# Late score step: sixteen pooled products of 32 columns first, the local products behind them

## The chip, the cores and the metric

The kernel runs on one core of one Trainium2 chip. The metric is device time in microseconds of one execution; the median of three runs is compared. Five engines matter: TensorE (PE, with its weight loads shown apart as PEld), VectorE (DVE), ScalarE (ACT), GpSimd (POOL), and SyncE (SP), which here only starts DMAs.

## The reference

Inputs q, k and v are 8 batches x 8 heads x 576 positions x 64. For each head there are two attentions that are added, and a feed-forward layer follows:

```
q_d, k_d, v_d = means over groups of 4 positions        # 144 pooled positions
out_d     = softmax(q_d k_d^T / 8) v_d                  # 144 x 144 scores, repeated 4 times
out_local = softmax(q k^T / 8 where |i - j| < 4) v      # a band of 7 positions
x = out_up + out_local                                  # 4608 tokens x 512
out = (h * cos(h)) @ w_out,  h = x @ w_in               # 512 -> 2048 -> 512
```

## The kernel before, in words

Most of the time goes to the feed-forward layer. It works on 12 tiles of 384 tokens and 16 blocks of 128 hidden units, with every float32 operand split into two float16 parts; line 1574 (and line 1499 later in the program) is its first product, line 1594 its second. Between those products stand the attention steps, one unit for each of 8 batches and 4 pairs of heads. Units of the first two batches are handled by other functions. The 24 units of batches 2 to 7 are "late" and have three steps each: scores (`late_s`), transposes (`late_t`) and the product with v (lines 1378 and 1385).

A late score step gets q and k of two heads (64 partitions each, so one head per half of the array's rows), and `qkd`, the sums of q and of k over groups of four positions, 144 of each. It computes into two PSUM banks, one per head:

- 48 local products at line 1071: 24 segments of 24 queries, each 32 query columns (stationary) by 32 key columns (moving), for two heads. Each falls on a piece of the array of 64 rows x 32 columns.
- 4 pooled products at line 1078: for each head all 144 pooled queries against 144 keys. The stationary operand has at most 128 columns, so the 144 queries are covered by two products, `i = 0` and `i = 1`, of 128 columns each. They overlap: of the second only the last 32 queries of a head are used, and the column offset is shifted by 32 for the second head so that these land on other partitions (`P - 32..P` for head 0, `64..96` for head 1).

All operands are float32. A float32 product is shown in the trace as two LDWEIGHTS and two MATMUL records, so 48 products are 96 records and 4 are 8.

The readers of the two banks stand on VectorE: line 1087 adds the band mask to the local scores, line 1101 takes the maxima of the pooled scores, line 1097 subtracts them. `late_t` then transposes the pooled weights (line 1130) and sends them through DRAM with small DMAs of SyncE (line 1135 and the line behind it). The next q and k are loaded by line 814 on SyncE's queue into the buffers that a score step has read; there are two of each.

The order on every engine is written out ahead of time by a planner (class `Plan`). It gives each operation a cost in us, simulates the engines, and disturbs the order by a table of seeds (`PICKS`). The score step is one operation for it, of cost 1.55 and with `num=209` instructions; neither number changes here. What a function like `mm` issues inside one operation is not the planner's matter.

Of the kernel before, what the change touches and what calls it, by code (L numbers as in the profile page):

```python
# [28 lines left out]
P = 128  # L29
# [11 lines left out]
SD = S // 4  # L41
# [3 lines left out]
BQ, BS = 24, 32  # L45
# [12 lines left out]
REM = SD - P  # L58
# [460 lines left out]
def _dve(n):  # L519
    return n * 0.001042 + 0.065  # L520
# [7 lines left out]
def attn_ffn_kernel(ctx: ExitStack, tc: tile.TileContext, qT, kT, vdn, vl, w_in, w_out, out, small):  # L528
# [4 lines left out]
    pe, act, dve, pool, sp = nc.tensor, nc.scalar, nc.vector, nc.gpsimd, nc.sync  # L533
# [9 lines left out]
    def sb(tag, n, shape, dtype=F32, name=None, pool=None):  # L543
        t = pl.turn(tag, n)
        if small and t in GUEST:
            k, c, off = GUEST[t]
            host, size = words[(k, c)], math.prod(shape[1:])
            pl.rings.setdefault(t, host)

            def make():  # L550
                half = host.get().rearrange("p f t -> p (f t)")[:, DM:].bitcast(dtype)
                return half[:shape[0], off:off + size]
            return pl.buf(make, t)
        return pl.buf(lambda: (pool or ap).tile(shape, dtype, name=name or tag, tag=t, bufs=1), t)
# [227 lines left out]
    def ub(b, pr, name):  # L782
        shape, n, chunk, off = UNIT[name]
        if b >= NEARLY and name in ("ptd", "vd4", "vd"):
            shape = [KH[0]] + shape[1:]
        if b == 1 and pr and name in "qk":

            own = cut(xx[1], 584 * (name == "k"), shape) if pr == 1 else \
                cut(wx[{(2, "q"): ("o", 8), (2, "k"): ("i", 7), (3, "q"): ("o", 7), (3, "k"): ("o", 6)}[(pr, name)]], 0, shape)
            return own  # L790
        if b < NEARLY and pr:
            return cut(wx[OWN[5 * (NPAIR - 1 - pr) + chunk]], off, shape)
        return sb({"ptl": "sml", "xs": "vd4"}.get(name, name), 2 if name == "ptl" else n, shape)

    def bank(b, kind):

        if b == 0:
            tags = ("pa.0", "po.0", "pa.1", "po.1") if kind == "s" else ("ph.0", "ph.1", "pa.2")
            return psum(tags[int(pl.turn("early" + str(kind == "s"), len(tags))[-1])])
        return psum(pl.turn("pa", 3) if b < NEARLY else pl.turn("pa", 2))  # L800
# [246 lines left out]
    def late_s(b, pr, u, q, k, qkd):  # L1047


        banks = [bank(b, "s") for _ in range(2)]  # L1050
# [7 lines left out]
        sml, smd = ub(b, pr, "sml"), pl.buf(lambda: prob, "prob")  # L1058
        loc, poo = [pl.buf(None) for _ in banks], [pl.buf(None) for _ in banks]

        def using(bk, o):
            bk.r.append(o)
            bk.acc.append(o)

        def mm():
            for f in range(2):
                for n in range(NSEG):
                    for g in range(4):
                        h = (g // 2 + f) % 2
                        hs, o, c = slice(64 * h, 64 * h + 64), (4 * n + g) * BQ, LQ + BS * n  # L1070
                        pe.matmul(banks[h].get()[BS * g:BS * (g + 1), c:c + BS],  # L1071
                                  q.get()[hs, o:o + BS], k.get()[hs, o:o + BS], start=True, stop=True)
            for i in range(2):
                for h in range(2):
                    hs = slice(64 * h, 64 * h + 64)
                    at = (SD - P + BS * h) * i
                    few = qkd.get()[hs].rearrange("p a n -> p (a n)")[:, at:at + P]
                    pe.matmul(banks[h].get()[:, i * SD:(i + 1) * SD], few, qkd.get()[hs, 1, :], start=True, stop=True)  # L1078
        pl.op("PE", 1.55, mm, r=[q, k, qkd], pw=banks, w=loc + poo, slack=SLACK, num=209)

        mxl, su, nl = sb("mxl", 2, [P, 2 * NSEG]), sb("su", 2, [P, 2 * NSEG + 3]), 2 * NSEG
        n = 2 * NSEG * BS
# [12 lines left out]
        def less(h, out, cols, r, lo, hi, **kw):  # L1095
            n = (cols.stop - cols.start) * SD
            using(banks[h], pl.op("DVE", _dve(n), lambda: dve.tensor_tensor(
                out=out(), in0=dq(h)[lo:hi, cols], in1=mxd.get()[lo:hi, h, cols].unsqueeze(2).broadcast_to([hi - lo, n // SD, SD]),
                op=ALU.subtract), r=[poo[h], mx[h]] + r, pw=[smd], **kw))
# [3 lines left out]
        wide0 = pl.buf(None)  # L1103
        less(0, lambda: smd.get()[:, 0::2, :SD], slice(0, 2), [], 0, P, w=[wide0])
        less(1, lambda: smd.get()[:, 1:2, :SD], slice(0, 1), [], 0, P)
        less(1, lambda: smd.get()[2 * BS:3 * BS, 2:3, :SD], slice(1, 2), [wide0], 2 * BS, 3 * BS)
        m = 3 * SD
        ds = lambda: smd.get()[:, :, :SD]

# [15 lines left out]
    def late_t(b, pr, u):  # L1125

        sml, smd = u["sml"], u["smd"]
        ptl, ptd, trn = ub(b, pr, "ptl"), ub(b, pr, "ptd"), sb("smd", 1, [P, 3, SD + REM], name="trn")
        scr = sb("scr", 2, [2, SD + REM, SD], pool=dr)
        pl.op("DVE", _dve(3 * (SD + REM)), lambda: dve.transpose(trn.get().rearrange("p s q -> p (s q)"),  # L1130
                                                                smd.get().rearrange("p s n -> p (s n)")), r=[smd], w=[trn])

        def out_():
            for g in range(4):
                sp.dma_start(scr.get().rearrange("h (j k) q -> k (h j) q", k=BS)[:, :, BS * g:BS * (g + 1)],
                             trn.get()[BS * g:BS * (g + 1), :2].rearrange("p h (j q) -> p (h j) q", q=BS))
            for h in range(2):
                sp.dma_start(scr.get()[h, :, P:].rearrange("(j k) q -> k j q", k=BS),
                             trn.get()[BS * (3 - h):BS * (4 - h), 2].rearrange("p (j q) -> p j q", q=BS)[:, :, BS - REM:])

        def in_():
            for i, lo in enumerate((0, KH[0])):
                sp.dma_start(ptd.get()[:KH[i], i], scr.get()[:, lo:lo + KH[i]].rearrange("h k q -> k h q"))
        pl.op("SP", 6 * 0.55, out_, r=[trn], w=[scr], lat=2.2)
        pl.op("SP", 2 * 0.55, in_, r=[scr], w=[ptd], lat=3.8)
        pl.op("DVE", _dve(2 * NSEG * BS), lambda: dve.transpose(ptl.get().rearrange("p s q -> p (s q)"),
                                                                sml.get().rearrange("p s n -> p (s n)")), r=[sml], w=[ptl])
        u["ptb"] = pl.buf(lambda: ptb, "ptb")

        def move():  # L1150
            for g in range(4):
                sp.dma_start(ptb[BS * g:BS * (g + 1), g % 2], ptl.get()[BS * g:BS * (g + 1)])
        dma(8 * P * NSEG * BS, move, r=[ptl], w=[u["ptb"]])
        u["ptl"], u["ptd"] = ptl, ptd

    def u_s(b, pr, part=None):
# [5 lines left out]
        if b >= NEARLY:  # L1162
            return late_s(b, pr, u, q, k, qkd)
# [632 lines left out]
```

## Time and profile before

| what | before |
|---|---|
| three runs, us | 905.36, 907.74, 912.56; median 907.74 |
| the profiled execution, its own time | 906.36 us |
| its span, first to last instruction | 904.4 us |
| granted TensorE clock, mean | 0.998 |
| PE busy | 876.5 us, 97% |
| DVE, ACT, POOL busy | 724.8, 625.5, 451.9 us |
| chain that ended last | PE 58%, DVE 14%, ACT 11%, POOL 4% |
| code fetched for PE | 84 packets, 1.38 MB |

The busy time of an engine is a union of its records, so it does not tell how well a busy PE is used. The chain that ended last is followed back from the last instruction: what stands on it sets the end, as far as the profile's semaphores tell. Records of one line that overlap are merged into one row in the timeline, with the time from the first start to the last end; the start of the row behind it tells when the engine went on.

### The profile page before, as it was taken

The numbers are of one execution on the slowest core, as the hardware profiler recorded it, in microseconds if no ns is written. First come the engines' busy times: TensorE is split into PE (matmuls) and PEld (weight loads), VectorE is DVE, ScalarE is ACT, GpSimd is POOL, SyncE is SP. The second block draws the span as 40 slices with busy tenths as digits, with TensorE's granted clock in tenths as the row PEclk, the third lists the DMA queues.
The fourth block names the chain that finished last, engine by engine and source line by source line (L and its number), as shares of the span: only waits on it lengthen the run. The fifth ranks groups of instructions, "written<-read, shape, count | busy, mean of one in ns | idle before, by whom it ended". The sixth has DMA issues, their size and how long they took to land.

```text
span 904.4 us, 26251 instructions
## 1 busy us (share of the span) xinstructions
PE 876.5 (97%) x10488; PEld 575.2 (64%) x10488; DVE 724.8 (80%) x1596; ACT 625.5 (69%) x1370; POOL 451.9 (50%) x563
## 2 busy tenths in 40 slices
PE   8989899999999999999999999999999999999996
PEld 4745555455555555777776667677776677777773
DVE  6889887999886959877789889977789878857662
ACT  3889999956666566566676766676686776655653
POOL 4694754557664636544367626533347534522221
PEclk9999999999999999999999999999999999999999
DMA  7893285115364731322424532334454421224501
GB/s 231 257 294 88 92 283 202 42 40 96 86 142 118 151 99 63 96 52 74 130 70 118 145 105 87 89 93 121 134 129 119 116 62 55 79 75 141 175 1 40
DMA packets 100853, 103.80 MB, mean 115 GB/s; under 512 B 47280, under 2 KB 73648, under 8 KB 100720
## 3 DMA queue, kind: packets, MB, share of 16 engines
q1 hardware_dynamic: 99280, 99.40, 37.5%
q0 software_dynamic: 1296, 2.36, 1.9%
q8 instruction: 84, 1.38, 0.6%
q14 instruction: 49, 0.40, 0.2%
q10 hardware_dynamic: 144, 0.26, 0.1%
HBM read 81.05 MB, written 16.22 MB: 108 GB/s over the span
## 4 chain that ended last, share of the span: by engine, by line
PE 58%; DVE 14%; ACT 11%; POOL 4%; issue 3%; DMA 1%; DVEq 0%; SPq 0%; ACTq 0%; POOLq 0%
PE bank L1594 27%; PE bank L1499 17%; PE bank L1574 8%; DVE rec L1415 3%; PE bank L1071 2%; PE bank L1385 2%; PE bank L1378 1%; ACT xxh L730 1%; PE bank L1078 1%; ACT tr L1554 1%; DVE tr L1555 1%; POOL wdo L678 1%; ACT L1554 1%; DVE tr L1552 1%; ACT xxh L726 1%
## 5 line engine op out<-in xcount | busy, mean ns | idle before, releaser
L1499 PEld LDWEIGHTS <-wdi 128*128 128x128 f16 x2400 | 204.3, 98 | 58.1 <-issue 4.1
L1594 PE MATMUL bank<-wdo,gh 128*128 128x512 f16 x696 | 207.1, 379 | 0.0
L1499 PE MATMUL bank<-wdo,wdi 128*128 128x192 f16 x1344 | 141.0, 246 | 2.1 <-DVE wdo L1520 1.4
L1594 PE MATMUL bank<-wdo,gl 128*128 128x512 f16 x348 | 131.7, 379 | 0.1
L1574 PEld LDWEIGHTS <-wdi 128*128 128x128 f16 x768 | 73.9, 98 | 58.8 <-issue 2.4
L1594 PEld LDWEIGHTS <-gh 128*128 128x128 f16 x696 | 64.0, 98 | 41.3 <-issue 0.2
L1594 PE MATMUL bank<-wdo,wdi 128*128 128x512 f16 x342 | 86.6, 379 | 0.7 <-ACT wdi L1612 0.7
L1554 ACT ACTIVATE tr<-tr,quarter 128x384 f32<-128x384 f32 x98 | 59.8, 613 | 39.3 <-DVE tr L1552 38.9
L678 POOL TENSOR_TENSOR gl<-tr,gh 128x384 f16<-128x384 f32 x51 | 49.9, 978 | 73.6 <-ACT gh L1557 39.4
L1594 PE MATMUL bank<-wdo,wdo 128*128 128x512 f16 x315 | 79.8, 379 | 1.5 <-ACT ob L1612 1.5
L1594 PEld LDWEIGHTS <-gl 128*128 128x128 f16 x348 | 34.1, 98 | 41.5 <-POOL gl L678 0.6
L1594 PEld LDWEIGHTS <-wdo 128*128 128x128 f16 x342 | 32.2, 98 | 29.0 <-issue 2.0
L1594 PEld LDWEIGHTS <-wdi 128*128 128x128 f16 x342 | 32.3, 98 | 28.4 <-issue 2.1
L1551 ACT ACTIVATE tr<-bank 128x384 int32<-128x384 f32 x66 | 31.6, 479 | 21.9 <-DVE bank L1515 16.9
L1555 DVE SCALAR_TENSOR_TENSOR tr<-tr,bank 128x384 f32<-128x384 f32 x66 | 35.9, 544 | 13.2 <-ACT tr L1554 13.1
L1415 DVE TENSOR_TENSOR rec<-rec 128x128 f32<-128x128 f32 (+1 forms) x98 | 44.3, 456 | 1.9 <-POOL rec L1415 0.7
L1515 DVE TENSOR_TENSOR bank<-bank,wdo 128x384 f32<-128x384 f32 x64 | 35.7, 558 | 12.0 <-PE bank L1499 11.7
L1554 ACT ACTIVATE wdo<-wdo,quarter 128x384 f32<-128x384 f32 x47 | 28.8, 613 | 20.8 <-DVE wdo L1552 20.6
L1121 POOL TENSOR_TENSOR blocks<-blocks,su 128x432 f32<-128x432 f32 x22 | 21.1, 959 | 43.8 <-DVE su L1118 37.6
L678 POOL TENSOR_TENSOR wdo<-rec,wdo 128x384 f16<-128x384 f32 (+1 forms) x34 | 34.1, 1010 | 17.5 <-ACT wdo L1460 16.4
L678 POOL TENSOR_TENSOR gl<-wdi,gh 128x384 f16<-128x384 f32 x26 | 25.2, 969 | 32.4 <-ACT gh L1557 22.7
L1554 ACT ACTIVATE wdi<-wdi,quarter 128x384 f32<-128x384 f32 x47 | 28.8, 613 | 17.4 <-DVE wdi L1552 17.2
(421 smaller groups left out, 2349.9 us busy)
## 6 DMA issues: line engine op xcount, KB each, us to landing
vl<-vl SPq DMA_DIRECT2D x26, 384.0 KB, 3.4
vd<-vdn SPq DMA_DIRECT2D x24, 384.0 KB, 4.7
wdi<-w_in SPq DMA_DIRECT2D x16, 512.0 KB, 5.6
wdo<-w_out SPq DMA_DIRECT2D x16, 512.0 KB, 7.1
again<-w_in SPq DMA_DIRECT2D x32, 256.0 KB, 4.8
again<-w_out SPq DMA_DIRECT2D x32, 256.0 KB, 3.6
q<-qT SPq DMA_DIRECT2D x26, 292.0 KB, 3.6
k<-kT SPq DMA_DIRECT2D x26, 292.0 KB, 4.2
```

The source lines that it names most:

```text
L678: f = lambda e: lambda: e.tensor_tensor(out=out(), in0=in0(), in1=in1(), op=ALU.subtract)
L1071: pe.matmul(banks[h].get()[BS * g:BS * (g + 1), c:c + BS], q.get()[hs, o:o + BS], k.get()[hs, o:o + BS], start=True, stop=True)
L1121: f = lambda e, get=get, by=by: lambda: e.tensor_tensor(out=get(), in0=get(), in1=by(), op=ALU.mult)
L1385: pe.matmul(banks[e].get()[64 * h:64 * h + 64, o:o + 2 * BQ], v4[r, NSEG * h + n, :], pt[r, :, NSEG * h + n, :BQ], start=True, stop=True)
L1415: f = lambda e: lambda: e.tensor_tensor(out=out(), in0=in0(), in1=in1(), op=op)
L1499: pe.matmul(bank.get()[:, half * HT:(half + 1) * HT], w(i, a), x(l, a), start=start and k == 0, stop=k == 5, skip_group_check=not start)
L1515: pl.op("DVE", _dve(TT), lambda: dve.tensor_tensor(out=by.get()[:, :TT], in0=by.get()[:, :TT], in1=s.get(), op=ALU.add), r=[mid, s], w=[by])
L1551: pl.op("ACT", _act(m, banked), lambda: act.activation(turns(), h(), AF.Copy, scale=1.0 / fm.h, bias=0.25), r=r, w=[tr])
L1554: pl.op("ACT", _act(m, False, 1), lambda: act.activation(tr.get(), tr.get(), AF.Sin, scale=-2.0 * PI / fm.h, bias=quarter), w=[tr], tab="sin")
L1555: pl.op("DVE", _dve(m), lambda: dve.scalar_tensor_tensor(out=tr.get(), in0=tr.get(), scalar=-0.5 * fm.ratio, in1=h(), op0=ALU.mult, op1=AL ...
L1574: pe.matmul(ph.get()[:, :m], w[:, i, kc, :], x[:, kc, :], start=(n == 0), stop=(n == 3 * KC - 1))
L1594: pe.matmul(o, (gh, gh, gl)[k].get()[:, sl], wo.get()[:, (0, 1, 0)[k]], start=(c == c0 and k == 0), stop=(c == c1 - 1 and k == 2))
```

## The change

In `late_s` the pooled products come first and are cut differently: for each head, four of 32 stationary columns cover the first 128 queries, and four more, all with the same last 32 queries, stand for the second range. That makes 16 products, each on a piece of the array of 64 rows x 32 columns, the same pieces that the local products use. The 48 local products follow, unchanged. Since the last 32 queries now lie on all four groups of partitions, head 1's are taken from partitions 32 to 63 and head 0's from 0 to 31, and `late_t` sends them from there.

```diff
         def mm():
+            for i in range(2):
+                for g in range(4):
+                    for h in range(2):
+                        hs, at = slice(64 * h, 64 * h + 64), SD - BS if i else BS * g
+                        pe.matmul(banks[h].get()[BS * g:BS * (g + 1), i * SD:(i + 1) * SD], qkd.get()[hs, 0, at:at + BS], qkd.get()[hs, 1, :],
+                                  start=True, stop=True)
             for f in range(2):
                 for n in range(NSEG):
                     for g in range(4):
...
-            for i in range(2):
-                for h in range(2):
-                    hs = slice(64 * h, 64 * h + 64)
-                    at = (SD - P + BS * h) * i
-                    few = qkd.get()[hs].rearrange("p a n -> p (a n)")[:, at:at + P]
-                    pe.matmul(banks[h].get()[:, i * SD:(i + 1) * SD], few, qkd.get()[hs, 1, :], start=True, stop=True)
...
-        less(1, lambda: smd.get()[2 * BS:3 * BS, 2:3, :SD], slice(1, 2), [wide0], 2 * BS, 3 * BS)
+        less(1, lambda: smd.get()[BS:2 * BS, 2:3, :SD], slice(1, 2), [wide0], BS, 2 * BS)
...
-                             trn.get()[BS * (3 - h):BS * (4 - h), 2].rearrange("p (j q) -> p j q", q=BS)[:, :, BS - REM:])
+                             trn.get()[BS * h:BS * (h + 1), 2].rearrange("p (j q) -> p j q", q=BS)[:, :, BS - REM:])
```

On PE, the first late score step stands in the program as follows (`bank` is the PSUM target, `wdo` and `wdi` are weights of the feed-forward layer, `x2h` is a token tile; sizes are those of the stationary columns by the moving ones):

```order
 L1594 LDWEIGHTS wdo_876
 L1594 MATMUL bank<-wdo_659,wdo_876 128x512
-L1071 MATMUL bank<-k,q 32x32 [waits DMAHW6_49,DMAHW5_49,PE_49]
-L1071 MATMUL bank<-k,q 32x32
-L1071 MATMUL bank<-k,q 32x32 [waits PE_49]
-L1071 MATMUL bank<-k,q 32x32 x45
-L1078 MATMUL bank<-qkd 128x144 x4
+L1070 MATMUL bank<-qkd 32x144 [waits PE_49] x2
+L1070 MATMUL bank<-qkd 32x144 x14
+L1077 MATMUL bank<-k,q 32x32 [waits DMAHW6_49,DMAHW5_49]
+L1077 MATMUL bank<-k,q 32x32 x47
 L1574 LDWEIGHTS wdi_1227
 L1574 MATMUL bank<-x2h,wdi_1227 128x384 [waits DVE_49]
```

The pooled products moved ahead of the local ones and take over their wait for the banks; the wait for the loads of q and k stays with the local products. What stands ahead of the step and behind it is the same, and so it is in all 24 steps.

On DVE, the readers of the two banks behind that step stand in the old order (`xxh` and the `wd` names belong to the feed-forward layer). Before:

```order
L1087 TENSOR_TENSOR sml<-bank,band 128x192 [waits PE_49]
L1101 TENSOR_REDUCE mxd<-bank 128x2
L1087 TENSOR_TENSOR sml<-bank,band 128x192 [waits PE_49]
L1097 TENSOR_TENSOR blocks<-bank,mxd 128x2x144 [waits DVE_49]
L742 SCALAR_TENSOR_TENSOR wdo_2096<-xxh,wdo_2096 128x512 [waits Activation_49]
```

And now:

```order
L1087 TENSOR_TENSOR sml<-bank,band 128x192 [waits PE_49]
L1101 TENSOR_REDUCE mxd<-bank 128x2
L1087 TENSOR_TENSOR sml<-bank,band 128x192
L1097 TENSOR_TENSOR blocks<-bank,mxd 128x2x144 [waits DVE_49]
L742 SCALAR_TENSOR_TENSOR wdo_2096<-xxh,wdo_2096 128x512 [waits Activation_49]
```

No row moved; one wait for PE fell away, because the first wait now covers it.

## Rows read from the trace of the kernel before

**Rows 1.** The page, part 1: span, then busy time and share of the engines.

```profile
span 904.4 us, 26251 instructions
PE 876.5 (97%) x10488; PEld 575.2 (64%) x10488; DVE 724.8 (80%) x1596; ACT 625.5 (69%) x1370; POOL 451.9 (50%) x563
```

**Rows 2.** The page, part 4: the chain that ended last, by engine.

```profile
PE 58%; DVE 14%; ACT 11%; POOL 4%; issue 3%; DMA 1%; DVEq 0%; SPq 0%; ACTq 0%; POOLq 0%
```

**Rows 3.** That chain between 140 and 760 us, by line.

```profile
by line: PE bank L1594 27.2%; PE bank L1499 15.7%; PE bank L1574 9.8%; issue 4.1%; DVE rec L1415 3.5%; PE bank L1071 2.5%; PE bank L1385 2.2%; PE bank L1378 2.1%; PE bank L1078 1.7%; ACT xxh L730 1.4%; DVE tr L1555 1.4%; ACT tr L1554 1.1%; 
```

**Rows 4.** Timeline of PE, 144:151 (start us, us, instruction).

```profile
145.40 1.02 PE L1071 MATMUL bank<-k,q 64*32 64x32 f32 x96
146.36 0.76 PE L1078 MATMUL bank<-qkd 64*128 64x144 f32 x8
147.05 0.34 PE L1574 MATMUL bank<-x2h,wdi 128*128 128x384 f16 x1
```

**Rows 5.** Lines 1071 and 1078: records, ns min/median/max, first and last start.

```profile
L1071 PE MATMUL bank<-k,q x2304: 186/193/213, 145.4 to 727.8; 64*32 64x32 f32 x192
L1078 PE MATMUL bank<-qkd x192: 282/283/387, 146.4 to 728.4; 64*128 64x144 f32 x192
```

**Rows 6.** Timeline of PE, 8.6:9.5 and 44.3:45: pooled products of early units.

```profile
8.75 0.71 PE L1194 MATMUL bank<-qkd 64*72 64x144 f32 x8
9.40 0.34 PE L891 MATMUL bank<-mask,ident_b 128*128 128x192 bf16 x2
...
44.52 0.45 PE L941 MATMUL bank<-qkd 64*48 64x144 f32 x4
44.90 0.39 PE L1737 MATMUL bank<-ident_b 128*128 128x512 bf16 x1
```

**Rows 7.** Timeline of PE, 304:306: a late step's product with v.

```profile
304.43 0.74 PE L1378 MATMUL bank<-ptd,vd 96*64 96x144 f32 x6
304.84 0.33 PE L1385 MATMUL bank<-blocks,vl 64*64 64x48 f32 x4
304.99 0.29 PE L1378 MATMUL bank<-ptd,vd 48*64 48x144 f32 x2
305.12 0.85 PE L1385 MATMUL bank<-blocks,vl 64*64 64x48 f32 x44
```

**Rows 8.** Timeline of DVE, 384:387, behind the step at 384.02 (idle time in brackets).

```profile
385.76 0.62 DVE L1087 TENSOR_TENSOR sml<-bank,band 128x192 f32<-128x192 f32 x2 [0.16 <-PE bank L1078]
386.30 0.45 DVE L1101 TENSOR_REDUCE mxd<-bank 128x2 f32<-128x288 f32 x1
```

**Rows 9.** Waits of SyncE's queue: us in total, times, longest.

```profile
SPq L814 <- PE bank L1071: 65.7, 13, 15.8
```

**Rows 10.** The chain that ended last, 477:484, in order of time.

```profile
478.44 0.37 DVE wdo L1520
...
478.85 0.66 PE bank L1499 x6
...
481.94 0.97 PE bank L1071 x66
...
482.93 0.33 SPq L814
...
483.30 3.60 DMA k<-kT
```

**Rows 11.** The page, part 3: the queue of PE's code (packets, MB, share).

```profile
q8 instruction: 84, 1.38, 0.6%
```

**Rows 12.** Timeline of PE, 690.5:694.6.

```profile
690.84 1.02 PE L1071 MATMUL bank<-k,q 64*32 64x32 f32 x96
...
692.83 0.25 PE L1499 MATMUL bank<-x0l,wdi 128*128 128x192 f16 x1
694.07 0.24 PE L1499 MATMUL bank<-x0h,wdi 128*128 128x192 f16 x1 [1.00 <-issue]
694.15 0.81 PE L1594 MATMUL bank<-wdo,wdi 128*128 128x512 f16 x3
```

## The prediction

> **What bounds the kernel now.** I read the page's busy times first: PE is busy for 876.5 of 904.4 us, DVE for 724.8 [rows 1]. A union of overlapping records says little about how well PE is used, so the chain of waits decides: 58% of it is PE, 25% DVE and ACT [rows 2]. The change touches 24 score steps between 145 and 728 us [rows 5], so the next view is the chain in that stretch, by line. There line 1078, the four pooled products, holds 1.7% of 620 us, which is 10.5 us [rows 3]. One step spends 147.05 - 146.36 = 0.69 us on them [rows 4], so 10.5 / 0.69 = 15 of the 24 steps lie on the chain. In the other nine DVE, ACT or POOL run later than PE, and a PE that gets done sooner there only waits longer at the next barrier. An example is the matmul at 478.85, which starts when DVE's line 1520 ends [rows 10].
>
> The last view is the timeline of one step: local products from 145.40 to 146.36 (0.96 us), pooled ones to 147.05 (0.69), 1.65 us together [rows 4].
>
> **The change, part by part.**
>
> *The price of a pooled record.* Two early units run pooled products against the same 144 columns. Eight records of 72 stationary columns take 9.40 - 8.75 = 0.65 us, four of 48 take 44.90 - 44.52 = 0.38 us [rows 6]. Both run the two heads in the two halves of the array's rows; if those go side by side, the first is four records deep and the second two, and a record costs (0.65 - 0.38) / 2 = 0.135 us. The late step fits: eight records, four deep, 4 x 0.135 = 0.54, and 0.15 for the first weight load and the emptying of the array, 0.69 in all. One after the other, eight would take 1.08.
>
> *The new pooled products.* Sixteen products are 32 records on eight pieces of the array (two row halves, four column groups), four per piece. If all eight pieces run side by side, they take 4 x 0.135 = 0.54 us. No row of before shows eight pieces at work on long operands; the nearest are the local products, whose 32 columns go to the same pieces. At 0.96 us for 96 records, 0.010 us each, though a record of 144 columns costs 0.135 and so one of 32 columns some 0.03, at least three pieces work at once there, of which at most two in a half. This gives both ends: eight pieces at once 0.54 us; two pieces in a half at a time 1.08 us, if a half of the array is fed no more than that. Nothing shown excludes the better end, and row halves that share nothing are shown [rows 4, 6], so I take 0.54.
>
> *The local products.* Same 48, same order, same pieces: 0.96 us including the change to what follows. They now end the step, and the emptying of the array that the pooled products paid at the end is paid by them. Pieces start one behind the other, at most 7 x 0.010 = 0.07 us late for the last; the local products follow in a similar order, so I add 0.03.
>
> *The step.* 0.54 + 0.96 + 0.03 = 1.53 against 1.65: 0.12 us less. What goes is one change of shape in mid-step and the load of 128 weight columns that nothing covered. With both ends: 0.19 less (pooled 0.50, since part of the 0.135 may be the wider load of the 72 columns, and no lag) to 0.46 more (pooled 1.08, full lag). On the chain, 15 x 0.12 = **-1.8 us**; the other nine steps give nothing.
>
> *Waits and queues.* PE's wait for the banks moves to the first pooled product, with nothing queued between the old place and the new. On DVE the first reader of a bank waits until the step has ended even now: in the step at 384.02 it starts at 385.76, 0.09 us after the end of a step of 1.65, released by line 1078 [rows 8]. It starts with the step's end afterwards too; that the local scores come last costs nothing there.
>
> SyncE is another matter. The loads of the next q and k wait for the local products of an earlier step, 13 times, 65.7 us in all [rows 9]. These products ended 0.96 us into the step and will end at 1.53, so such loads, and what is queued behind them, start up to 0.57 us later. A load is covered where its use is far off; once it stands on the chain: at 482.93 line 814 is released by the local products, the load takes 3.60 us and DVE goes on behind it [rows 10]. Part of this is regained by steps that started earlier: **+0.4 us**.
>
> *Six small DMAs per step* are issued as before with the same bytes, two from other partitions, and DVE's 32-partition subtraction has the same size: nothing, covered by the transposes and loads of a whole unit.
>
> *Code.* A step issues 12 more products, 4 x 12 = 48 more PE instructions; 24 steps add 1,152 to the 20,976 of the page. They come in 84 packets, 250 instructions each [rows 1, 11], so five packets more. In the trace one step is followed by an idle PE that waits for nothing shown: at 694.07, 1.00 us, behind the step at 690.84 [rows 12]. I read it as code that came late: the step has 208 instructions in 1.65 us, which is most of a packet, while three products of the feed-forward layer, six instructions, take 0.81 us [rows 12]. Now it has 256 in less time, and every packet falls elsewhere. Lower end: the one stall goes away, -1.0. Upper end: one step in three stalls, 8 x 1.0 = 8. I take one more stall, **+1.0 us**, as a single one in 24 steps is nearest. The Trainium skill, Runtime: NRT & Kernel Launch, section Instruction fetch mechanics, says that crossing a block of 256 instructions costs something "mostly hidden"; by that rule alone this term would be near 0, and the idle time in rows 12 is the exception to it.
>
> *The sum.* -1.8 + 0.4 + 1.0 = -0.4 us on the profiled execution's 906.36: 906.0. The median of the three runs, 907.74, stands 1.4 above that execution, so I forecast **907.3 us** for the changed kernel's median: no change that can be told.
>
> **The rivals.**
>
> *A: strict order across pieces.* If a record could not start before the one ahead of it in the program, the second record of a product would wait for the first, and the next product would wait with it. Then sixteen products take (16 + 1) x 0.135 = 2.3 us instead of 0.54, 1.76 more than in my sum. A step on the chain loses 1.64, 15 lose 25 us, and with the nine others, whose slack would be used up, 24 lose 39; with the other terms 934 to 949, taken at **938 us**. It decides from the first step on. Against it: in the product with v, line 1378 stands ahead of line 1385 in the program, yet four records of line 1385 start at 304.84, before the last two of line 1378 at 304.99 [rows 7]; and four pooled products would have taken 5 x 0.135 + 0.15 = 0.83 rather than 0.69 [rows 4]. The skill, TensorE: Matmul & The Clock Gate, section Part 2: What happens when you issue a matmul, holds this rule: matmuls "stay in program order" and only weight loads are pulled ahead. By it the time is that of this rival; the trace disagrees at the rows named, where pieces differ. Chance 4%.
>
> *B: a half of the array is fed by two pieces at a time.* Pooled products take 1.08, a step 0.42 more than before: 15 x 0.42 = 6.3, with the other terms 7.7 more: **915 us**. For it: rows of before never show more than two per half. Against it: nothing measured. Chance 13%.
>
> *C: code comes late in many steps.* The saving stays, but every third step stalls: 8 x 1.0 in place of 1.0: **914 us**. For it: the stall in rows 12 and the larger burst. Against it: one stall in 24 so far. Chance 15%.
>
> *D: the better ends together.* Each step saves 0.19 on the chain and the stall goes away: 15 x 0.19 + 1.0 = 3.9 less, and SyncE's later loads stay covered: **904 us**. Chance 13%.
>
> *E: the change does not do what it says.* The order on PE shows the sixteen products first in all steps, so there is nothing to weigh: 0%.
>
> **How the numbers follow.** My forecast holds 55%. The three runs spread over 7 us, 0.8%, and about 1% is what a measurement of this kernel can tell from none. Under 898.7 us (1% less) no case lies: 2%. Over 916.8: A, and the upper parts of B and C, 8%. Within: 90%. The range of 901 to 915 takes in D with some spread of the runs, the forecast, and the middle of B and C; A and the upper parts of B and C are left out.
>
> **What would show it.** In the changed trace a step should read 0.54 to 0.6 us from the first record of line 1070 to the first of line 1077, and 1.5 us to the row behind the step. If the first of these is 1.1, B holds; if it is 2.3, A. The eight pieces should show as groups of up to eight records that start within 0.1 us. More idle PE with no releaser, a microsecond or so behind a step, would be C. The chain should hold fewer steps of PE and more of DVE and ACT. I am wrong if the steps save 0.3 us or more each, or if SyncE's later loads push the q and k sums onto the chain in several places.

## The result, and the profile after

| what | before | changed |
|---|---|---|
| median of 20 runs of each, us | 909.32 (905.36 to 913.33) | 915.11 (912.40 to 918.20) |
| ratio, 95% interval | | 1.0063 (1.0047 to 1.0080) |
| span of the profiled execution, us | 904.4 | 910.6 |

The changed kernel is 5.8 us slower. The forecast was 907.3, 0.4 us faster than before on the profiled execution; the sign is wrong, and 915.11 lies just past the range.

The page of the changed kernel answers to [rows 1], [rows 11] and [rows 2]: 576 matmul records more, five packets of code more, and PE as busy as before in a span that is 6.2 us longer.

```profile
span 910.6 us, 27391 instructions
PE 876.4 (96%) x11064; PEld 576.7 (63%) x11064; DVE 724.3 (80%) x1596; ACT 625.8 (69%) x1370; POOL 451.3 (50%) x563
...
q8 instruction: 89, 1.46, 0.7%
...
PE 55%; DVE 17%; ACT 11%; POOL 4%; issue 4%; DMA 1%; SPq 0%; DVEq 0%; ACTq 0%; POOLq 0%
```

The step itself came out as forecast. PE's timeline of the first late step in the changed kernel, to be read beside [rows 4]:

```profile
143.52 0.72 PE L1070 MATMUL bank<-qkd 64*32 64x144 f32 x32
144.03 1.07 PE L1077 MATMUL bank<-k,q 64*32 64x32 f32 x96
145.03 0.34 PE L1574 MATMUL bank<-x2h,wdi 128*128 128x384 f16 x1
```

Sixteen pooled products take 144.03 - 143.52 = 0.51 us; their 32 records start in four groups of eight, at 143.52, 143.66, 143.79 and 143.91, each group within 0.05 us. The step takes 1.51 to 1.55 in 20 of the 24 places, against 1.65. So PE saved some 20 x 0.12 = 2.4 us and still ended 6.2 later. Where it went is seen by setting the same piece of work side by side in both traces: the changed kernel is 1.9 us ahead at the first late step (143.52 against 145.40, before the change has done anything), 1.84 ahead at the step at 288.22 (290.06 before), 0.4 ahead at 310.48, and **6.7 behind** at 356.25 (349.53 before). Then nothing moves any more: 6.2 behind at 733.15 (726.95) and at the end. The loss is made between 310 and 356.

PE's timeline there, changed kernel (idle time before a row, and what ended it, in brackets):

```profile
310.48 0.73 PE L1070 MATMUL bank<-qkd 64*32 64x144 f32 x32 [0.68 <-DVE vd L1394]
310.96 1.11 PE L1077 MATMUL bank<-k,q 64*32 64x32 f32 x96
312.01 0.39 PE L1594 MATMUL bank<-wdo,gh 128*128 128x512 f16 x1
317.33 0.59 PE L1594 MATMUL bank<-wdo,gh 128*128 128x512 f16 x1 [4.93 <-issue]
317.70 0.63 PE L1594 MATMUL bank<-wdo,gl 128*128 128x512 f16 x1
318.13 0.53 PE L1574 MATMUL bank<-x3h,wdi 128*128 128x384 f16 x1
...
321.65 0.37 PE L1574 MATMUL bank<-x3h,wdi 128*128 128x384 f16 x1
321.86 0.38 PE L1594 MATMUL bank<-wdo,gh 128*128 128x512 f16 x1
```

And the same work before:

```profile
310.89 1.01 PE L1071 MATMUL bank<-k,q 64*32 64x32 f32 x96 [0.28 <-issue]
311.84 0.76 PE L1078 MATMUL bank<-qkd 64*128 64x144 f32 x8
312.53 0.60 PE L1594 MATMUL bank<-wdo,gh 128*128 128x512 f16 x2
...
315.14 0.59 PE L1594 MATMUL bank<-wdo,gh 128*128 128x512 f16 x2
```

One product behind the step, PE stands idle for 4.93 us and waits for nothing that the profile shows. After that it is slow: the products of line 1574 start 0.32 us apart (318.13, 318.45 and so on) instead of 0.16. From the end of the step to the next products of line 1594 pass 321.86 - 312.01 = 9.85 us, where before it is 315.14 - 312.53 = 2.61. The stall costs 7.2 us: 4.93 of idle time and 2.3 at a lower clock. The windows of the changed kernel show the clock (columns: stretch, its length, PE busy, then the other engines, granted clock, DMA share, GB/s):

```profile
312.40:317.30 4.90, 0.00 (x0) 0.00 (x0) 3.76 (x11) 0.65 (x2) 2.73 (x3) 0.75 0.71 134
317.30:319.50 2.20, 2.17 (x7) 0.95 (x7) 0.00 (x0) 0.00 (x0) 0.00 (x0) 0.50 0.30 66
319.50:321.80 2.30, 2.30 (x9) 1.11 (x8) 0.00 (x0) 0.00 (x0) 0.00 (x0) 0.52 0.77 232
321.80:326.00 4.20, 4.20 (x25) 2.19 (x23) 2.32 (x5) 3.90 (x5) 1.69 (x3) 1.00 0.16 48
```

A granted clock of 0.50 is the lower of the two levels, 1.2 GHz. It fell while PE was idle (0.75 is the mean of that stretch) and stayed there for the first 4.4 us of work behind it. The Trainium skill, Advanced Engine Details and Errata, Clock Domains, says that the array's clock is gated to 1.2 GHz when idle; these rows agree as to the fall, and show that the lower level goes on into the work behind it. Not every idle PE brings it: behind 1.74 us (below) the clock stayed at 1.00.

What PE waited for can be read from the queue of its code. The window 314.7 to 315.7 holds the only packet between 312 and 317.3:

```profile
q8 instruction: 1, 0.02, 5.8%
```

In windows of 0.1 us it starts between 314.7 and 314.8, 2.6 us ahead of PE's next product. The 4.29 us from the step's start to the packet's start are the puzzle, since a packet is normally there long before it is needed.

To place the packets, I counted PE's instructions in the built programs (four for a float32 product, two for a float16 one) and marked every 256th, an "edge". 256 agrees with the 16 KB of a packet on the page (1.46 MB / 89) and with the planner's constant `BLOCK`. In the changed kernel an edge falls on instruction 65 of the 256 of the step at 310; before, on 139 of 208. PE stops at instruction 257 of this count, 192 past the edge. The planner assumes the same reach: its constant `FIRSTS`, 448, is 256 + 192. In the traces of all runs below taken together, twelve more stalls in or close behind a score step (0.42 to 4.37 us, the one at 694.07 in [rows 12] among them) begin within three instructions of edge + 192.

**The theory to be tested**: a packet is asked for when PE's sequencer comes to an edge. In this step the sequencer is held at the first product, until VectorE has read the bank (`DVE vd L1394`, which runs from 309.55 to 310.33, below), so the packet is asked for late; the transfers of that moment delay it further; and the code at hand ends 192 instructions past the edge, which is just behind a step of 256 instructions. **Rivals**: the order itself (pooled first, local last) delays VectorE and SyncE; or more code costs more, wherever it stands. VectorE's row in the changed kernel:

```profile
309.55 0.78 DVE L1394 TENSOR_TENSOR vd<-bank,xd 128x288 f32<-128x288 f32 x2
```

### The profile page after: what moved, and what is told of

Its sections match the earlier page's. It is cut to its first block, busy times and chain, and to the rows that moved or that the text cites. A ratio compares the mean times of both kernels' runs of the same rounds, so it can differ in the third digit from the quotient of the medians.

```text
span 910.6 us, 27391 instructions
## 1 busy us (share of the span) xinstructions
PE 876.4 (96%) x11064; PEld 576.7 (63%) x11064; DVE 724.3 (80%) x1596; ACT 625.8 (69%) x1370; POOL 451.3 (50%) x563
## 3 DMA queue, kind: packets, MB, share of 16 engines
q8 instruction: 89, 1.46, 0.7%
## 4 chain that ended last, share of the span: by engine, by line
PE 55%; DVE 17%; ACT 11%; POOL 4%; issue 4%; DMA 1%; SPq 0%; DVEq 0%; ACTq 0%; POOLq 0%
PE bank L1594 26%; PE bank L1499 17%; PE bank L1574 6%; DVE rec L1415 3%; PE bank L1077 2%; PE bank L1385 1%; PE bank L1378 1%; ACT xxh L730 1%; PE bank L1070 1%; ACT tr L1554 1%; DVE tr L1555 1%; DVE tr L1552 1%; POOL wdo L678 1%; ACT L1554 1%; DVE blocks L1097 1%
```

## Experiments

All runs are compared with the kernel before on the same chip. Line numbers shift where lines were added.

**The two halves of the change.** First the order alone:

```diff
         def mm():
+            for i in range(2):
+                for h in range(2):
...
+                    pe.matmul(banks[h].get()[:, i * SD:(i + 1) * SD], few, qkd.get()[hs, 1, :], start=True, stop=True)
             for f in range(2):
...
-                    pe.matmul(banks[h].get()[:, i * SD:(i + 1) * SD], few, qkd.get()[hs, 1, :], start=True, stop=True)
```

> The four wide pooled products of before, only moved ahead of the local ones; the code has the length of before, so every packet of code ends at the same instruction as before. Theory (a late code packet behind the step at 310 makes the whole loss): no idle PE behind that step, the old 1.00 us stall behind the step at 691 stays; a step takes 1.50 to 1.65 us; time 0 to 2 us below before, ratio 0.998 to 1.000. Rival 1 (the order itself, pooled first and local scores last, delays VectorE and SyncE): the loss of the change shows here too, +5 us, ratio 1.005.

Measured: 908.71 us, ratio 0.9992 (0.9970 to 1.0014). The steps take 1.65 us, so the order saves nothing at all; no stall at 310 and, against expectation, none at 694 either. The code is not quite that of before: it has a few waits fewer, and counted in the built program the edge in the step behind which PE stalled at 694 stands at 34 instead of 25, and its packet starts 0.42 us ahead of that step, where it was 0.67 behind. Then the split alone:

```diff
             for f in range(2):
...
-                    pe.matmul(banks[h].get()[:, i * SD:(i + 1) * SD], few, qkd.get()[hs, 1, :], start=True, stop=True)
+            for i in range(2):
+                for g in range(4):
+                    for h in range(2):
...
+                        pe.matmul(banks[h].get()[BS * g:BS * (g + 1), i * SD:(i + 1) * SD], qkd.get()[hs, 0, at:at + BS], qkd.get()[hs, 1, :],
```

> Sixteen narrow pooled products behind the local ones: the length of code of the change without its order. Theory: the packet's edge in the step at 310 lies where it lies in the changed kernel, so PE idles 4.5 to 5 us behind that step, waiting for nothing shown; ratio to before 1.004 to 1.007. Rival 1 (the order does it): no such idle time, ratio 0.998 to 1.001.

Measured: 915.06 us, ratio 1.0061 (1.0035 to 1.0087), as much as the whole change. PE's timeline:

```profile
313.38 0.74 PE L1077 MATMUL bank<-qkd 64*32 64x144 f32 x29
318.48 0.44 PE L1077 MATMUL bank<-qkd 64*32 64x144 f32 x1 [4.37 <-issue]
318.86 1.04 PE L1594 MATMUL bank<-wdo,gh 128*128 128x512 f16 x2
```

The edge lies at 59 here, so the code at hand ends at 251, inside the step, and PE stops in front of the last pooled record that the trace shows. This run has a second stall, 1.57 us at 282.62 inside the step at 279.46, which the changed kernel has not. The order is refuted as the cause; the split both saves the 0.13 us and brings the loss.

**A stall made in the kernel before.** The local products of one early step are issued a second time (the same result to the same place), which moves all later edges and, but for 0.5 us in that step, nothing else:

```diff
+            for n in range(30 if (b, pr) == (2, 0) else 0):
...
+                pe.matmul(banks[h].get()[BS * g:BS * (g + 1), c:c + BS],
+                          q.get()[hs, o:o + BS], k.get()[hs, o:o + BS], start=True, stop=True)
```

> The kernel before, with 30 of the local products of the first late step (the one at 145 us) issued a second time: 120 instructions more, some 0.6 us, nothing else. All later edges of code packets stand 120 instructions earlier in the program. Theory: in the step at 310 the edge falls on instruction 19 instead of 139 of 208, so the code at hand ends about with the step, and PE idles about 4.6 us behind it; the old 1.00 us stall at 694 goes away. Together +4 us, ratio 1.003 to 1.006. Rival 2 (more code in general costs: 1,152 instructions cost the change 6 us): 120 cost 0.6 us, with the products 1.2 us, ratio 1.001, and no new stall at 310.

Measured: 908.62 us, ratio 1.0000 (0.9982 to 1.0018). No stall at 310, although the edge stands at 19 of 208 there: the packet starts between 308.4 and 308.5, 3.5 us ahead of the step at 312.01. My expectation failed. If the sequencer is held there, a packet with its edge 19 instructions behind the product that waits is asked for all the same. The same with 27 products:

> The kernel before, with 27 of the local products of the first late step issued a second time: 108 instructions more, about 0.55 us. The edge in the step at 310 moves from instruction 139 to 31 of 208, and the code at hand ends 15 instructions behind the step, some 1.9 us. Theory: the packet starts 4 us behind VectorE's release, as in the changed kernel, and PE idles 2 to 3 us, about 2 us behind the step; the 1.00 us stall at 694 goes away; ratio to before 1.001 to 1.003. Rival (31 can still be reached while the step waits): no stall, ratio 0.999 to 1.001.

Measured: 908.66 us, ratio 0.9999 (0.9982 to 1.0016); no stall, edge at 31, packet between 307.8 and 307.9, 4.1 us ahead of the step at 311.92. In both runs 108 and 120 more instructions cost nothing that can be told; the change adds 1,152, so the rival "more code costs" is left to the next runs, which carry them all.

**The edge moved in the changed kernel**, by 12 and by 5 products issued twice in the step at 144:

```diff
+            for n in range(12 if (b, pr) == (2, 0) else 0):
...
+                pe.matmul(banks[h].get()[BS * g:BS * (g + 1), c:c + BS],
+                          q.get()[hs, o:o + BS], k.get()[hs, o:o + BS], start=True, stop=True)
```

> The changed kernel, with 12 of the local products of the first late step (at 144 us) issued a second time: 48 instructions more, about 0.25 us. The edge of the code packet in the step at 310 moves from instruction 65 to 17 of 256. Theory (a packet asked too late, because PE's sequencer is held at the first product of the step until VectorE has read the bank, and can look only a little way past it): in the run of before with 30 second products the packet with its edge at instruction 19 started 3.5 us ahead of the step, so here too it starts ahead of the step, and the 4.93 us at 317 are gone; time 5 us below the changed kernel, ratio to before 0.998 to 1.001. Rival 2 (more code in general, or the padding, costs): ratio 1.006 or more.

Measured: 910.15 us, ratio 1.0010 (0.9992 to 1.0028). Edge at 17, packet 3.8 us ahead of the step, no stall at this place.

> The changed kernel, with 5 of the local products of the first late step issued a second time: 20 instructions more, about 0.1 us. The edge in the step at 310 moves from instruction 65 to 45 of 256. Theory: 45 is still too far behind the product that waits (59 was, in the run with the split alone), so the stall stays, 4.5 to 5.1 us, since the code at hand now ends 19 instructions ahead of the end of the step; ratio to before 1.005 to 1.007. Rival (any shift of the code removes it, or padding helps in another way): the stall is gone, ratio 1.000.

Measured: 908.52 us, ratio 1.0008 (0.9982 to 1.0033). The stall is gone here too, against my expectation. PE's timeline (line 1400 is 1394 of the changed kernel, 1600 is 1594):

```profile
312.04 0.72 PE L1070 MATMUL bank<-qkd 64*32 64x144 f32 x32 [0.68 <-DVE vd L1400]
312.52 1.11 PE L1077 MATMUL bank<-k,q 64*32 64x32 f32 x96
313.57 0.60 PE L1600 MATMUL bank<-wdo,gh 128*128 128x512 f16 x2
314.01 0.38 PE L1600 MATMUL bank<-wdo,gl 128*128 128x512 f16 x1
```

The step waits 0.68 us for VectorE exactly as in the changed kernel, but with the edge at 45 the packet starts between 309.5 and 309.6, 2.5 us ahead of the step. Twenty instructions that do nothing new take the loss away. This decides against both rivals, since the step and its order are those of the changed kernel and the code is a little longer. It also goes against the theory's own forecast, by which the packet of an edge at 45 would be as late as that of 65; what is left of the theory is the place of the edge and the 192 instructions past it.

The other direction, 20 instructions fewer, by the old pooled products in the step at 144:

```diff
+            if (b, pr) == (2, 0):
...
+                        pe.matmul(banks[h].get()[:, i * SD:(i + 1) * SD], few, qkd.get()[hs, 1, :], start=True, stop=True)
+            else:
...
+            for n in range(7 if (b, pr) == (2, 0) else 0):
...
```

> The changed kernel, where the first late step (at 144 us) has the four wide pooled products again and 7 of its local products a second time, so that it has 20 instructions fewer than in the change. The edge of the code packet in the step at 310 moves from instruction 65 to 85 of 256, and the code at hand ends 21 instructions behind the step instead of 1; these are ten products of the feed-forward layer, some 2 us. Theory: PE runs on past the step for about 2 us and then idles for 2 to 3 us instead of 4.9; ratio to before 1.002 to 1.005. Rival (any other place of the code is harmless): no idle time, ratio 1.000.

Measured: 912.89 us, ratio 1.0042 (1.0020 to 1.0064). PE's timeline (1610 and 1590 are 1594 and 1574):

```profile
314.44 0.72 PE L1078 MATMUL bank<-qkd 64*32 64x144 f32 x32 [0.67 <-DVE vd L1410]
...
315.97 0.60 PE L1610 MATMUL bank<-wdo,gh 128*128 128x512 f16 x2
...
317.76 0.33 PE L1590 MATMUL bank<-x3l,wdi 128*128 128x384 f16 x1
319.83 0.48 PE L1590 MATMUL bank<-x3h,wdi 128*128 128x384 f16 x2 [1.74 <-issue]
320.15 0.32 PE L1590 MATMUL bank<-x3l,wdi 128*128 128x384 f16 x1
```

PE now runs through eleven products behind the step, where ten were forecast (21 instructions), and idles 1.74 us. Behind it the products stand 0.17 us apart and the clock stays at 1.00 (columns as above): the second part of the price falls away with the shorter stall.

```profile
319.80:322.00 2.20, 2.17 (x12) 1.08 (x12) 0.94 (x3) 1.30 (x2) 0.36 (x1) 1.00 0.30 76
```

Two more stalls (0.74 us at 284.75, 0.99 at 668.86) make up most of the rest of this run's loss.

**The transfers.** GpSimd's output transfers, which add into the output, are cut to a sixteenth:

```diff
-                    pl.op("POOL", 1.0, lambda dst=dst, ob=ob: pool.dma_start(dst, ob.get(), accum_op=ALU.add),
+                    pl.op("POOL", 1.0, lambda dst=dst, ob=ob: pool.dma_start(dst[:8], ob.get()[:8], accum_op=ALU.add),
```

> The changed kernel; the nine output transfers that GpSimd issues to add into the output write 8 of their 128 rows, so part of the output lacks its second half. Theory with transfers: the code packet behind the edge at 311 started 3.8 us late because the DMA engines were full of these transfers; with them gone it starts about 1.2 us behind the edge as elsewhere, and the idle time at 317 falls from 4.9 to 2 to 2.5 us; ratio to before 1.003 to 1.004. Rival 3 (the delay has nothing to do with these transfers): 4.5 to 5 us of idle time stay, ratio 1.006.

Measured: 909.69 us, ratio 1.0017 (0.9993 to 1.0040).

```profile
312.35 0.72 PE L1070 MATMUL bank<-qkd 64*32 64x144 f32 x32
...
315.33 0.38 PE L1594 MATMUL bank<-wdo,gh 128*128 128x512 f16 x1 [1.05 <-issue]
```

The stall falls to 1.05 us, further than forecast, and two things changed at once. The packet starts 1.7 us behind VectorE's release (310.73 to 312.46) instead of 4.4 (310.33 to 314.77) or, in the split alone, 3.8 (312.32 to 316.08). But the release came earlier as well: VectorE's line 846 takes 0.88 us at 307.52 here, and 3.50 at 305.01 in the changed kernel, so the bank is free 1.6 us ahead of the step. The run does not separate the two any further, and why line 846 got shorter stays open; that the transfers made the packet late is not shown.

The same trace has another stall of 1.05 us, in the step at 279.86:

```profile
280.38 1.17 PE L1077 MATMUL bank<-k,q 64*32 64x32 f32 x90
282.60 0.26 PE L1077 MATMUL bank<-k,q 64*32 64x32 f32 x6 [1.05 <-issue]
```

PE's code is that of the changed kernel, with the edge at 50 of 256 in this step. There the packet starts 3.30 us ahead of the step (at 277.35) and PE does not stop; here it starts 0.55 behind it. So from one run to another the same edge can fall on either side.

The step at 310 over these runs (edge: at which instruction of how many; packet: its start against the start of the step):

| run | edge | packet, us | idle, us | ratio |
|---|---|---|---|---|
| with 12 twice | 17 of 256 | -3.8 | 0 | 1.0010 |
| before, 30 twice | 19 of 208 | -3.5 | 0 | 1.0000 |
| before, 27 twice | 31 of 208 | -4.1 | 0 | 0.9999 |
| with 5 twice | 45 of 256 | -2.5 | 0 | 1.0008 |
| split alone | 59 of 256 | +3.5 | 4.37 | 1.0061 |
| changed kernel | 65 of 256 | +4.3 | 4.93 | 1.0063 |
| light output | 65 of 256 | +0.1 | 1.05 | 1.0017 |
| 20 fewer | 85 of 256 | +3.2 | 1.74 | 1.0042 |
| before | 139 of 208 | +4.2 | 0 | 1 |
| order alone | 145 of 208 | +3.9 | 0 | 0.9992 |

In this step the packet comes ahead of it up to an edge at 45, and from 59 on behind it. Behind it, PE idles if the code at hand, edge + 192, ends in the step or close behind it. In a step of 208 an edge at 59 would leave 43 instructions behind the step, in one of 256 it ends inside it; no run put the old step's edge between 31 and 139, so how much safer the old step is here is not shown. It is not immune, as the stall at 694 in [rows 12] tells. What is special here is how late the packet comes: at the other steps of these traces the packet of an edge between 59 and 145 starts somewhere from 3.1 us ahead of the step to 2.0 behind its start (+0.73 with an edge at 73 at 446.22 in the run with 12 twice, which costs a stall of 0.42 us), and in this one 3.2 to 4.3 behind, but for the run with light output.

**Ten products**, with the second range in two wide products and only the first range split:

> Ten pooled products: the second range in two wide products as before, first, then the first range in eight narrow ones, then the local products; 24 instructions more per step instead of 48, so the edge in the step at 310 falls on instruction 227 of 232. Theory: no stall there, a step takes 1.52 to 1.60 us; ratio to before 0.997 to 1.001. Rival 2 (more code in general): half of the loss of the change, ratio 1.003.

Measured: 909.64 us, ratio 1.0007 (0.9987 to 1.0028). No stall, but a longer step. (Counted in the built program the edge stands at 233, just behind the step of 232, not inside it at 227.) PE's timeline at its first place:

```profile
147.10 0.52 PE L1071 MATMUL bank<-qkd 64*128 64x144 f32 x4
147.54 0.48 PE L1075 MATMUL bank<-qkd 64*32 64x144 f32 x16
147.81 1.07 PE L1082 MATMUL bank<-k,q 64*32 64x32 f32 x96
148.81 0.34 PE L1579 MATMUL bank<-x2h,wdi 128*128 128x384 f16 x1
```

Two wide products take 0.44 us, eight narrow ones 0.27, the local ones 1.00: 1.71 us together. It has a use all the same: a step 0.06 us longer than before gives the same time as one that is 0.12 shorter (the runs with 12 and 5 twice).

**A new order for the new step.** The planner weighs late code by `num`, which the change left at 209. Told the true length, and given other seeds that it judged better for it (it drops 51 of 96 and adds 7):

```diff
-        pl.op("PE", 1.55, mm, r=[q, k, qkd], pw=banks, w=loc + poo, slack=SLACK, num=209)
+        pl.op("PE", 1.55, mm, r=[q, k, qkd], pw=banks, w=loc + poo, slack=SLACK, num=257)
-PICKS = (...)
+PICKS = (...)
```

> The changed kernel, with the step's true length told to the planner (num=257 in place of 209) and 52 other seeds that change the order of the work on all engines, chosen for that length by the planner's own accounts. The step at 310 has its edge at instruction 83, where the planner holds it harmless, and 25 steps' lengths and places shift. Theory: if the planner's rule for code were the chip's, no stall over 1 us and the saving of 0.13 us a step gives ratio 0.997 to 1.000; if what the chip showed so far decides (a packet asked behind the release, 4 us late there), a stall of 2 to 3 us stays behind that step, ratio 1.002 to 1.004.

Measured: 898.72 us, ratio 0.9876 (0.9844 to 0.9908), better than both expectations: 1.2% faster than before, and no idle PE without a cause over 0.71 us behind the first late step. In this order the packet of the step's edge (79 in the built program) starts 0.75 us behind the step's start at 308.85, not 3 to 4, and PE does not stop. To see whose gain this is, the same order with the old step:

> The kernel before, its score step untouched, but with the seeds and the length (257) given to the planner in the run that came out at 0.988: the order of all operations on all engines is that of that run, only the step is the old one, 208 instructions. Theory (the gain came from the new order, and the change of the step gives at most 0.6 us by itself): ratio to before 0.986 to 0.991. Rival (the change of the step lets this order work: 24 x 0.13 = 3 us more on the path): ratio 0.991 to 0.995. If the order needs the new step altogether: 1.000.

Measured: 897.48 us, ratio 0.9866 (0.9837 to 0.9895). So the order alone makes the gain, and the new step adds nothing that can be told. The first two lines of its page and its chain, old step in the new order:

```profile
span 894.3 us, 26280 instructions
PE 874.3 (98%) x10487; PEld 575.2 (64%) x10487; DVE 714.9 (80%) x1585; ACT 628.8 (70%) x1374; POOL 458.2 (51%) x569
...
PE 75%; ACT 6%; DVE 5%; issue 1%; DMA 0%; POOL 0%; SPq 0%; DVEq 0%; ACTq 0%; POOLq 0%
```

PE holds 75% of the chain instead of 58 [rows 2]: what the order took out are waits for DVE and ACT. In a chain like this a shorter step ought to count in full, 24 x 0.13 = 3.1 us or 0.003, yet the two runs in this order can't be told apart (0.9876 and 0.9866, intervals that overlap nearly wholly and that leave room for the 3 us). In the profiled executions 752.6 us pass from the first late step to the end with the new step, and 753.0 with the old one. In each PE stands idle once for over 0.25 us behind the first late step and waits for nothing shown; first the new step's, then the old step's:

```profile
295.30 0.73 PE L1364 MATMUL bank<-ptd,vd 96*64 96x144 f32 x6 [0.71 <-issue]
```

```profile
685.78 0.26 PE L1485 MATMUL bank<-x0h,wdi 128*128 128x192 f16 x1 [1.11 <-issue]
```

The old step has the longer of the two, so they don't explain why the shorter step gives so little here, and that stays open. And other seeds for the kernel before, at its own length:

> The kernel before, with seeds from the same search, run as long and with the old length of 209: the planner's own account falls only from 872.96 to 872.78, but VectorE's, ScalarE's and GpSimd's work stands in another order. Theory (other orders differ by some us on the chip, and the planner's account does not tell which): ratio anywhere from 0.990 to 1.006. Rival (the search itself brings the 1.2% whatever the step): ratio 0.986 to 0.990.

Measured: 903.46 us, ratio 0.9926 (0.9901 to 0.9951), for a gain of 0.02% by the planner's account. So a search at the old length gives 0.7% too; that the true length makes the rest of the 1.2% is not shown, since each is a single order. The fastest version is the new order, with either step.

## Why the prediction was wrong

- **The price of the products** was right: 0.51 us measured for the sixteen (0.54 forecast), 1.51 to 1.55 for a step (1.53). Rivals A (2.3 us) and B (1.08) are refuted by the first timeline above.
- **"15 of the 24 steps lie on the chain, -1.8 us"** failed. Without the stall the changed kernel stands at 1.0008 and 1.0010, no gain, where 1.8 us would be 0.998. In the traces the time saved turns into waiting at the next wait for VectorE. The product behind the step at 481.87 before, and behind the one at 488.11 in the changed kernel, shows it:

```profile
484.19 0.24 PE L1499 MATMUL bank<-x1h,wdi 128*128 128x192 f16 x1 [0.60 <-DVE wdi L1555]
```

```profile
490.42 0.24 PE L1499 MATMUL bank<-x1h,wdi 128*128 128x192 f16 x1 [0.70 <-DVE wdi L1555]
```

From the step's start to this product pass 484.19 - 481.87 = 2.32 us before (the first row) and 490.42 - 488.11 = 2.31 after: the step is 0.10 us shorter and the wait 0.10 longer. I had set steps off the chain at nothing, but a step on the chain also ends, some steps later, at such a barrier, and what was saved up to there is lost if VectorE is nearly as late. From 478.85 (485.09 after) to 726.95 (733.15) PE gained 0.04 us over nine steps, where the forecast's own share, 15 of 24 at 0.12 us, would be 0.7.

- **The stall at 694 in [rows 12]** went away as the lower end of the code term assumed, and gave nothing: from the step at 690.84 to that at 726.95 pass 36.11 us before, and 36.08 in the changed kernel (697.07 to 733.15). Its two waits for VectorE there grew from 0.27 to 0.61 + 0.76 us.
- **Code, "+1.0 us, one more stall"**, is the step that failed. The mechanism was the right one, code that comes late behind a step, but its price was wrong. I took 1.0 us from the one stall in [rows 12] and set rival C's 8 us as eight stalls of that size. The new stall took 4.93 us and another 2.3 through the clock, 7.2 in all. The count was not quite right either: the new stall came in place of the one at 694, not beside it. What I could have seen in the trace of before is the packet's start: it starts at 315.0, 4.2 us behind the start of the step at 310.89, and by the count of 192 goes unpunished because the edge stands at 139 of 208. I also left unused what the kernel's planner assumes of late code (`FIRSTS`, `SEQ`, `FETCH`, `CROWD = 448, 105, 3.8, 1.0`, used in `burst`). By its constants a packet with its edge at 65, asked for at the release at 310.33, is there at some 314.4 to 315.4; PE runs out at 312.4, so my estimate from them is 2 to 3 us of idle time: nearer to 4.93 than 1.0, and still too low. Its rule would hold the packets of edges at 17 to 45 as well, which the runs refute. The count of packets was right (84 + 5 = 89). The Trainium skill, Runtime: NRT & Kernel Launch, Instruction fetch mechanics, calls the cost of a block's crossing "mostly hidden"; for nearly all of the 89 packets the trace agrees, and at 317.33 it does not.
- **SyncE, +0.4 us**: its waits for the local products grew from 65.7 us in 13 to 72.2 us in 14, as expected, but no place where this reached the end of the kernel was found.
- **Rival C** gave 914, near the 915.11 measured, by eight small stalls; it was one large one. That its time came near is luck. Its chance of 15% was too low as a chance of late code, because I weighed how often code had been late and not how late it was at the one place where the step waits for VectorE amid a burst of transfers.

The sum by the profiled executions: 7.2 us for the stall, 1.9 less from the different start before the first late step, 1.4 more from two waits between 288 and 310 (0.95 us before line 1378 at 295.43, and 0.40 longer at 310.48) that the run with 5 twice has only one of, and 0.5 less from 356 to the end, together the 6.2 between the spans. The start and the wait at 295 are taken as differences from run to run; the stall is not, since the split alone and the change have it and the two runs with the edge at 17 and 45 don't.

What stays open: what sets the reach between 45 and 59 instructions past the start of the step at 310 (it is no fixed count: near 280 an edge at 50 fell on either side, and the packet of the edge at 25 behind which PE stalled at 694 started 0.67 us behind its step), whether it is the wait for VectorE that holds the packet back at all (no run took it away alone), and how the 3.3 to 4.4 us from VectorE's release to the packet's start divide between the transfers and the fetch itself.

## What to carry to other kernels

A change that adds instructions to an engine that streams its code moves every later packet, so count where the edges fall in each burst of short instructions and look up when each packet started, not only whether it was late. A gain of 0.1 us per step on an engine that meets another every few steps can go into the next wait; another order of all the work was worth some 12 us here, the shorter step nothing that can be told in either order. Before a small loss or gain is believed of an edit, shift the code by a few harmless instructions and measure again.

## What the runs showed of the hardware

- Five products issued twice, 20 instructions 160 us ahead of the place, moved the time by half a per cent (1.0063 to 1.0008).
- Behind idle times of 4.93 and 4.37 us PE worked at a granted clock of 0.50 for 4.4 and 5.7 us; behind 1.74 us (at 319.83) it stayed at 1.00.
- Late code stopped PE within three instructions of 192 past an edge of 256, in thirteen stalls of 0.42 to 4.93 us.
- Eight pieces of the array, of 64 rows by 32 columns, run float32 products of 144 columns side by side: 32 records in 0.51 us, in four groups of eight.
- Wide products ahead of narrow ones lengthen the step: 1.71 us with ten products, 1.51 with sixteen narrow ones.
